# Six weight blocks of the closing MLP prepared at the hand-over instead of during the attention's second half

## The chip, the cores and the metric

The kernel runs on one core of one Trainium2 chip. The metric is the device time of one execution in microseconds (us). A core has TensorE for matmuls (PE in the profile, its weight loads PEld), VectorE (DVE), ScalarE (ACT), GpSimd (POOL) and SyncE (SP), which here only issues DMAs. Each engine works through its own instructions in the order in which they were written, and waits at an instruction until what it needs is there.

## The reference

Attention that keeps the 32 largest scores of each row, then a mixture of experts with one expert for each token, then an MLP with three weight matrices of which the largest product counts:

```
scores = scale * q @ k.T                        # 4 batches, 8 heads, 576 x 576, head size 64
kth    = 32nd largest of each row
attn   = softmax(where(scores >= kth, scores, -1e9)) @ v
x      = attn as [2304, 512]
out    = x;  for tokens with x @ w_skip > 0:  e = argmax(x @ w_gate)
         out += gate * (relu(x @ w1[e]) @ w2[e])            # 8 experts, 512 -> 1024 -> 512
h      = max(out @ m1, out @ m2, out @ m3)                  # 512 -> 768, given as 64-bit floats
y      = h @ m_out                                          # 768 -> 512
```

The weights m1, m2, m3 and m_out reach the chip as 64-bit floats.

## The kernel before

**Stages.** The tokens are worked in two parts of two batches. Attention is a run of 16 jobs (a batch and a pair of heads); each job is five units, a tail unit T of 64 rows for both heads and units 0 to 3 of 128 rows, and takes nine slots. Jobs 0 to 7 are part 0 (slots 0 to 71, `PART1` is 72), jobs 8 to 15 part 1 (slots 72 to 143, `NI` is 144). For each unit PE makes the scores (`scores2`), ACT copies half of them (`copy2`), DVE finds the 32nd largest (`search`, with `folds` and `finds`), ACT and POOL mask and take the exponential (`below`, `mask`, `expo`), PE transposes (`turn`) and multiplies with v (`av`). In part 0 the scores are one product and `scores2` puts two idle matmuls ahead of them (`warm`); in part 1 they are three products of split operands.

**What sets the order.** There is no scheduler. `at(i, o, fn)` puts a step into slot i at place o (0 to 99) and the steps are written out in that order. The table `WHEN`, one for each part, holds for each kind of step its distance in slots from its unit. `search` stands at place 40 of its slots, so the slots go by at the pace of DVE, or of what DVE waits for.

**Fillers.** From slot `b0` on, the expert products of part 0 are dealt out between the attention's steps (`experts`, `filler`): the first step of that list that PE does is `u_x`, which transposes the rows `xg` of the first expert. These rows are gathered by token: `route(0)` finds where each token goes, POOL scatters the rows to `xs` in DRAM (`scatter`), SP reads `xg` back. `BD` sets how many slots lie between the scatters and `b0`; `FLO` is the place in a slot at which the copies that the fillers have left over are made (`flush`).

**Preparation of weights.** The MLP's weights are 24 blocks of 128 x 512 values of 64 bits. `prep_load` brings one in; `prep` turns it into two fp32r tiles, a high and a low half: a square on ACT, four operations on DVE that build a 32-bit float out of the two words, and `split`, which rounds (on ACT) and subtracts (on POOL). `PREP0` and `PREPD` set at which slot the first block is prepared and how many slots lie between two. Blocks 0 to 11 are prepared in the attention's second half, 12 to 23 later.

**The hand-over.** When the attention ends, the first three token tiles of part 0 (`g00`) go on to the MLP: `g_load` gathers the experts' outputs (`yg<-ys`, a DMA that POOL issues once the last expert's output is in DRAM), `g_add` adds them on DVE (`x<-yg,gwc,x`), `g_in` transposes on PE and splits on ACT and DVE (x1h, x1l), and `g_l1` multiplies, with blocks 0 to 5 for its first two columns of blocks and 6 to 11 for the third. Then part 1 is routed, its experts run, and the MLP for the rest.

Of the kernel before, what the change touches and what calls it, by code (L numbers as in the profile page):

```python
# [31 lines left out]
PARTS_ENG = lambda nc: (nc.vector,) * 4  # L32
PARTS_AT = (1, 4, 6)
PARTS_LAST = (1, 0)
FLO = 25
FLE = 25
SPLIT = (1,)
NXR = 1
NLO = 2
SCT = 0.72  # L40
BD = 2
FO = [(50, 1), (90, 99)]
SOON = 0
SC0 = 4
# [2 lines left out]
NM0 = 12  # L47


WHEN = [  # L50
    {"trk": -7.7, "outk": -6.84, "trq": -5.82, "outq": -5.5, "below0": 1.19, "below1": 1.25, "mask0": 1.23,
     "mask1": 1.33, "exp0": 2.36, "exp1": 3.11, "norm": 2.64, "turnT": 3.52, "avT": 4.43, "outT": 5.49,
# [3 lines left out]
    {"trk": -6.4, "outk": -6.07, "trq": -5.4, "outq": -4.92, "below0": 1.15, "below1": 1.25, "mask0": 1.31,  # L56
     "mask1": 1.33, "exp0": 2.15, "exp1": 2.74, "norm": 2.65, "turnT": 3.51, "avT": 4.65, "outT": 5.0,
# [3 lines left out]
]  # L61
BF16 = mybir.dt.bfloat16
PREP0, PREPD, PREP_O = 18, 4, 42
DR_LD = (0, 32)
DR_ADD = (3, 42)
DR_IN = (4, 52)
DR_F = (0, 1, 2)
DR_FS = [(5, 58, 1), (6, 45, 2)]
C2 = (1.125 * 2.0 ** -15) ** 2
# [28 lines left out]
def body(ctx, tc, q, k, v, w_skip, w_gate, w1, w2, m1, m2, m3, m_out, out):  # L98
# [734 lines left out]
    def split(dsth, dstl, src, eng, rnd=None):  # L833
        if rnd:
            rnd.tensor_copy(dsth, src)
        else:
            A.copy(dsth, src)  # L837
        eng.tensor_tensor(dstl, src, dsth, op=ALU.subtract)
# [8 lines left out]
    def place(i, dt=F32):  # L847

        pool = env["M0" if i < NM0 else "M1"]
        Ms[i] = pool.tile([P, 2, 512], dt, name=f"M{i}", bufs=1)  # L850
        return Ms[i]

    def M(x, i):

        return Ms[i][:, x]
# [5 lines left out]
    def prep(i, alone=False):  # L861

        raw = Ms[i].rearrange("p x n -> p (x n)")
        words = raw.bitcast(I32).rearrange("p (n t) -> p n t", t=2)
        w = un.tile([P, 512], F32, name="pw", bufs=3)
        sq = un.tile([P, 512], BF16, name="psq", bufs=3)
        wi = w.bitcast(I32)


        return [  # L870
            lambda: A.activation(sq, raw.rearrange("p (n t) -> p n t", t=2)[:, :, 1], AF.Square),
            lambda: V.tensor_scalar(wi, words[:, :, 1], 5, 2, op0=ALU.logical_shift_left, op1=ALU.logical_shift_right),
            lambda: V.scalar_tensor_tensor(wi, words[:, :, 1], -1073741824, wi, op0=ALU.bitwise_and, op1=ALU.bitwise_or),
            lambda: V.scalar_tensor_tensor(wi, words[:, :, 0], 29, wi, op0=ALU.logical_shift_right, op1=ALU.bitwise_or),
            lambda: V.scalar_tensor_tensor(w, sq, C2, w, op0=ALU.is_ge, op1=ALU.mult),
            lambda: place(i, F32R),
            lambda: split(M(0, i), M(1, i), w, *((V, V) if alone else (G,)))]
# [34 lines left out]
    def g_l1(g, f, M):  # L912

        n = g.n
        pw = []

        def prod(i):
            if i == 0:
                pw.extend(mm3([n * P]))
            ps = pw[i]  # L920
            for c in range(4):
                j = (f // 2) * 6 + i * 2 + c // 2
                o = (c % 2) * 256 + (f % 2) * P
                gh = g.xh[:, c].rearrange("p a b -> p (a b)")[:, 0:n * P]
                gl = g.xl[:, c].rearrange("p a b -> p (a b)")[:, 0:n * P]
                T.matmul(ps, M(0, j)[:, o:o + P], gh, start=(c == 0), stop=False)  # L926
                T.matmul(ps, M(0, j)[:, o:o + P], gl, start=False, stop=False)  # L927
                T.matmul(ps, M(1, j)[:, o:o + P], gh, start=False, stop=(c == 3))  # L928

        def put():  # L930
            mv = env["m2a"].tile([P, GMAX * P], F32, name="mv", bufs=1)[:, 0:n * P]
            A.copy(mv, pw[0])
            V.tensor_max(mv, mv, pw[1])  # L933
            V.tensor_max(mv, mv, pw[2])  # L934
            pool = env["m2a" if f < 3 else "m2"]
            hh = pool.tile([P, GMAX * P], F32R, name=f"h2h{f}", bufs=1)
            hl = pool.tile([P, GMAX * P], F32R, name=f"h2l{f}", bufs=1)
            split(hh[:, 0:n * P], hl[:, 0:n * P], mv, V)
            g.h.append((hh, hl))
        return [lambda: prod(0), lambda: prod(1), lambda: prod(2), put]  # L940
# [29 lines left out]
    NI = i0  # L970
    PART1 = sum(J.n for J in jobs if J.part == 0)

    with tc.manual_schedule():
# [16 lines left out]
        def at(i, o, fn, *a):  # L990
            todo.setdefault(i, []).append((o, len(todo.get(i, [])), fn, a))

        ends = [jobs[-1], [J for J in jobs if J.part == 0][-1]]
        for J in jobs:
# [15 lines left out]
            for u in J.units:  # L1010
                i = z + J.tiles.index((u, 0))
# [45 lines left out]
        fill = experts([0, 1])  # L1057
        b0, b1 = r0 + SC0 + 1 + BD, NI + BX

# [25 lines left out]
        for i in range(b0, b1):  # L1085
            at(i, FLO if i < NI - 3 else FLE, flush)
            for fo, j in FO:
                at(i, fo, filler, i, j, fo == FO[0][0])
        at(2, 39, load_gate)
        def prep_at(i, z):  # L1090
            ops = []
            at(z, PREP_O - 1, lambda: ops.extend(prep(i)))
            for j in range(7):
                at(z + j // 2, PREP_O + j % 2, lambda j=j: ops[j]())

        for i in range(NM0):
            at(PART1 + PREP0 - 6 + PREPD * i, 5, prep_load, i)
            prep_at(i, PART1 + PREP0 + PREPD * i)
        m2a = []

        def turnover():
# [9 lines left out]
                    fsq.pop(0)()  # L1111

        at(NI, 50, turnover)
        at(NI + DR_ADD[0], DR_ADD[1], g_add, g00)
        at(NI + DR_IN[0], DR_IN[1], g_in, g00)
        at(NI + DR_IN[0], DR_IN[1] + 1, lambda: fsq.extend(x for f in DR_F for x in g_l1(g00, f, M)))
        for i, o, n in DR_FS:
# [216 lines left out]
```

## Time and profile before

| | |
|---|---|
| device time, median of 3 runs | 1092.09 us (1091.97 to 1093.41) |
| the profiled execution | 1092.1 us, span 1090.2 us |
| busy: PE, DVE, ACT, POOL | 980.3, 744.0, 592.0, 366.9 us |
| one job in part 0 (148.2 to 182.4 us) | 34.2 us, DVE busy 33.65 |
| attention's second half from the first expert's transposes to PE's last matmul | 361.6 to 639.1 us |
| hand-over, PE idle | 639.1 to 645.1 us |

A busy time is the sum of an engine's instructions as the profiler saw them, overlaps counted once. The granted clock is TensorE's: 1.00 stands for 2.4 GHz and 0.50 for 1.2 GHz, and a mean between them says that the stretch had both. "Idle before" an instruction is the time its engine stood still ahead of it, with the instruction or DMA whose end released it.

### The profile page before, as it was taken

To read this page: it belongs to the slowest core of one execution; us is meant where nothing else is said; L and a number is where in the kernel's file an instruction comes from. 1 tells how busy PE (TensorE), PEld (TensorE's weight loads), DVE (VectorE), ACT (ScalarE), POOL (GpSimd) and SP (SyncE) were. 2 spreads that over 40 slices of the span, in tenths; PEclk is the share of its full clock that TensorE was granted. 3 is DMA by queue.
4 is the path that set the end of the run, shared out by engine and by line. 5 is a ranking of instruction groups with operands and counts; after the bars stand their busy time and mean duration, and the time that the engine had idled before them with its cause. 6 is when DMAs were issued, how large, how long until landed. Compare 5 with 4: busy or idle time off the path is not lost. (4 is left out here: it accounts for less than half of the span.)

```text
span 1090.2 us, 19236 instructions
## 1 busy us (share of the span) xinstructions
PE 980.3 (90%) x6747; PEld 765.5 (70%) x6747; DVE 744.0 (68%) x2482; ACT 592.0 (54%) x1295; POOL 366.9 (34%) x484
## 2 busy tenths in 40 slices
PE   5987788888887889999999978889999999999996
PEld 2554455454554767767677758879889999999995
DVE  5999999999889789999999922774441313222221
ACT  3787878877875777977886831355321211121111
POOL 1444444544455654755654524020030101010000
PEclk8899999989877899999999979899999999999998
DMA  4110111101427566575574556899931111111001
GB/s 115 60 45 16 30 44 45 44 12 34 135 68 227 172 207 198 159 235 178 160 214 148 163 160 213 292 370 370 377 133 58 39 50 49 39 51 36 29 2 32
DMA packets 146154, 136.64 MB, mean 125 GB/s; under 512 B 64384, under 2 KB 110976, under 8 KB 146048
## 3 DMA queue, kind: packets, MB, share of 16 engines
q1 hardware_dynamic: 143168, 125.88, 36.7%
q0 software_dynamic: 2880, 9.44, 2.6%
q8 instruction: 55, 0.90, 0.3%
q14 instruction: 51, 0.42, 0.1%
HBM read 112.22 MB, written 23.07 MB: 124 GB/s over the span
## 5 line engine op out<-in xcount | busy, mean ns | idle before, releaser
L442 POOL TENSOR_TENSOR e<-sc,e 128x576 f32<-128x576 f32 x144 | 201.6, 1416 | 93.0 <-ACT e L437 91.5
L926 PE MATMUL pe<-x1h,M 128*128 128x384 f32 x432 | 145.8, 338 | 0.0
L928 PE MATMUL pe<-x1h,M 128*128 128x384 f32 x432 | 145.2, 336 | 0.0
L927 PE MATMUL pe<-x1l,M 128*128 128x384 f32 x432 | 145.2, 336 | 0.0
L475 PE MATMUL pe<-ident,e 128*128 128x128 f32 x624 | 106.4, 291 | 35.9 <-POOL e L460 16.1
L730 PE MATMUL pe<-xT,raw 128*128 128x128 f32 x1024 | 127.6, 280 | 1.7 <-ACT xT L719 1.1
L730 PEld LDWEIGHTS pe<-xT,raw 128*128 128x128 f32 x1024 | 121.4, 195 | 6.0 <-issue 2.8
L933 DVE TENSOR_TENSOR mv<-mv,pe 128x384 f32<-128x384 f32 x36 | 19.9, 554 | 151.9 <-PE pe L928 143.8
L475 PEld LDWEIGHTS pe<-ident,e 128*128 128x128 f32 x624 | 70.6, 145 | 74.9 <-ACT e L451 22.1
L437 ACT ACTIVATE e<-sc,sts 128x576 f32<-128x576 f32 x144 | 111.4, 779 | 16.1 <-POOL sts L418 15.9
L476 ACT COPY et<-pe 128x384 f32<-128x384 f32 x208 | 97.9, 480 | 39.2 <-PE pe L475 38.4
L451 ACT ACTIVATE e<-e,sts 128x576 f32<-128x576 f32 x144 | 113.6, 789 | 4.1 <-POOL e L442 4.0
L837 ACT CAST h2h<-mv 128x384 fp32r<-128x384 f32 x36 | 18.5, 514 | 147.8 <-DVE mv L934 141.9
L494 PE MATMUL pe<-et,ldv 128*64 128x128 f32 x1024 | 84.4, 294 | 7.0 <-ACT et L476 7.0
L418 POOL TENSOR_TENSOR sts<-g,stc 128x4 f32<-128x4 f32 (+1 forms) x80 | 20.2, 253 | 191.6 <-DVE g L395 170.1
L494 PEld LDWEIGHTS pe<-et,ldv 128*64 128x64 f32 x1024 | 64.5, 145 | 28.3 <-ACT et L476 19.5
L384 DVE MATCH_REPLACE8 g<-g 128x144 f32<-128x144 f32 x288 | 82.6, 293 | 0.0
L926 PEld LDWEIGHTS pe<-x1h,M 128*128 128x128 f32 x432 | 81.7, 189 | 0.5 <-issue 0.2
L927 PEld LDWEIGHTS pe<-x1l,M 128*128 128x128 f32 x432 | 81.6, 189 | 0.4 <-issue 0.2
L928 PEld LDWEIGHTS pe<-x1h,M 128*128 128x128 f32 x432 | 81.6, 189 | 0.0
L746 PE MATMUL pe<-raw,hT 128*128 128x512 f32 x160 | 78.5, 605 | 1.5 <-ACT et L476 1.0
L383 DVE MAX8 g<-g 128x8 f32<-128x144 f32 x288 | 74.9, 297 | 0.0
(223 smaller groups left out, 2044.6 us busy)
## 6 DMA issues: line engine op xcount, KB each, us to landing
raw<-in_moe_w_dram SPq DMA_DIRECT2D x128, 512.0 KB, 5.4
M<-in_moe_w_dram SPq DMA_DIRECT2D x18, 512.0 KB, 5.2
M<-xd SPq DMA_DIRECT2D x18, 256.0 KB, 5.4
x<-xd SPq DMA_DIRECT2D x18, 256.0 KB, 3.6
ldq<-in_q_dram SPq DMA_DIRECT2D x32, 128.0 KB, 3.3
ldk<-in_k_dram SPq DMA_DIRECT2D x32, 128.0 KB, 2.8
ldv<-in_v_dram SPq DMA_DIRECT2D x32, 128.0 KB, 2.6
xs<-zerob SPq DMA_DIRECT2D x16, 256.0 KB, 2.8
```

Of the source, the lines that this page charges most:

```text
L384: ops += [lambda h=h, o=o: V.match_replace(g[:, h, 0:QS], g[:, h, o:o + 8], g[:, h, 0:QS], NEG) for h in range(nh)]
L437: A.activation(J.w[i], J.sc[i], AF.Relu, bias=J.st[i][0], scale=-BIG)
L442: G.tensor_tensor(w, J.sc[i], w, op=ALU.subtract)
L451: A.activation(J.w[i], J.w[i], AF.Exp, bias=J.st[i][1], scale=0.125, accum_out=J.ss[:, j:j + 1])
L475: T.transpose(pe[:, i], e[:, 3 * g + i], ident)
L476: A.copy(et[:, 3 * g:3 * g + 3], pe[:, 0:3])
L494: T.matmul(xo[h * 64:(h + 1) * 64], vt[:, i, h, :], et[:, 5 * h + i], start=(i == 0), stop=False)
L730: T.matmul(u.ph[:, f], u.c1[2 * n + f // 2][:, c, (f % 2) * P:(f % 2 + 1) * P], u.xT[:, c], start=(c == 0), stop=(c == 3))
L746: T.matmul(u.py, x, w[:, ws], start=(c + a + j == 0), stop=(c + a == 4 and j == len(prods) - 1))
L926: T.matmul(ps, M(0, j)[:, o:o + P], gh, start=(c == 0), stop=False)
L927: T.matmul(ps, M(0, j)[:, o:o + P], gl, start=False, stop=False)
L928: T.matmul(ps, M(1, j)[:, o:o + P], gh, start=False, stop=(c == 3))
```

## The change

Blocks 0 to 5 stay in the attention's second half, every eighth slot instead of every fourth. Blocks 6 to 11 are loaded in slots 130 to 135 and prepared at the hand-over in two groups of three (`DR_PREP`, `pre`): the squares, then the four DVE operations, then place and split, with rounding and subtraction both on DVE (`prep(i, True)`). `g_in` comes one slot earlier (`DR_IN`), the fillers begin one slot earlier (`BD`), `flush` stands at place 15 instead of 25, and 30 numbers of `WHEN` move, among them in part 0 the third transposition of a unit (turn2), the tail's scores (s0T) and products (avT).

```
-FLO = 25
+FLO = 15
-BD = 2
+BD = 1
...
-     "turn0": 3.21, "turn1": 3.361, "turn2": 4.37, "av": 4.95, "rows1": 3.43, "rows2": 5.51, "rows3": 6.05,
+     "turn0": 3.21, "turn1": 3.361, "turn2": 3.52, "av": 4.95, "rows1": 3.93, "rows2": 5.51, "rows3": 5.97,
...
-PREP0, PREPD, PREP_O = 18, 4, 42
+PREP0, PREPD, PREP_O = 20, 8, 42
+DR_PREP = [[(-1, 12), (0, 42), (0, 43), 6, 9], [(2, 21), (2, 44), (3, 43), 9, 12]]
-DR_IN = (4, 52)
+DR_IN = (3, 52)
...
-        for i in range(NM0):
+        for i in range(6):
             at(PART1 + PREP0 - 6 + PREPD * i, 5, prep_load, i)
             prep_at(i, PART1 + PREP0 + PREPD * i)
+        for i in range(6, NM0):
+            at(NI - 20 + i, 5, prep_load, i)
+
+        def pre(a, b):
+
+            ops = []
+
+            def first():
+                ops.extend([prep(i, True) for i in range(a, b)])
+                for o in ops:
+                    o[0]()
+
+            def rest(rs):
+                for r in rs:
+                    for o in ops:
+                        o[r]()
+            return first, lambda: rest(range(1, 5)), lambda: rest((-2, -1))
+
...
+        for *places, a, b in DR_PREP:
+            for (i, o), fn in zip(places, pre(a, b)):
+                at(NI + i, o, fn)
```

**DVE at the hand-over.** Before, the last search (MAX) is followed at once by the three additions of `g_add`; rs and lt belong to the last job, x1l to `g_in`.

```order
L395 MAX g<-g 128x8 x2
L899 SCALAR_TENSOR_TENSOR x_8019<-yg,gwc_100,x_8019 128x512
L899 SCALAR_TENSOR_TENSOR x_8023<-yg,gwc_100,x_8023 128x512
L899 SCALAR_TENSOR_TENSOR x_8027<-yg,gwc_100,x_8027 128x512
L454 TENSOR_SCALAR rs<-ss 128x8
L455 RECIPROCAL rs<-rs 128x8
L838 TENSOR_TENSOR x1l<-pe,x1h 128x4x128 x3
```

In the changed program the whole of blocks 6 to 8 and the four operations of blocks 9 to 11 stand between the last search and the additions; here are the rows from the last of those operations on.

```order
L876 SCALAR_TENSOR_TENSOR pw<-psq,pw 128x512 x3
L900 SCALAR_TENSOR_TENSOR x_7987<-yg,gwc_100,x_7987 128x512
L900 SCALAR_TENSOR_TENSOR x_7991<-yg,gwc_100,x_7991 128x512
L900 SCALAR_TENSOR_TENSOR x_7995<-yg,gwc_100,x_7995 128x512
L836 CAST M_8052<-pw 128x512
L839 TENSOR_TENSOR M_8052<-pw,M_8052 128x512
L836 CAST M_8053<-pw 128x512
L839 TENSOR_TENSOR M_8053<-pw,M_8053 128x512
L836 CAST M_8054<-pw 128x512
L839 TENSOR_TENSOR M_8054<-pw,M_8054 128x512
L839 TENSOR_TENSOR x1l<-pe,x1h 128x4x128 x3
```

Thirty DVE operations moved ahead of the additions (three times four and three times two for blocks 6 to 8, three times four for 9 to 11), and six stand between the additions and x1l.

**PE at the first expert's transposes.** xg are the rows that SP reads back after the scatters; s and sa are score tiles. Before, two sets of scores, each behind its two idle matmuls on zerob, stand ahead of them, with the transposes of q (ldq) between the two sets; the second set and what follows are:

```order
L316 LDWEIGHTS zerob
L316 MATMUL sa<-zerob 128x512
L316 LDWEIGHTS zerob
L316 MATMUL sa<-zerob 128x512
L291 MATMUL sa<-kt,qt 128x288
L291 MATMUL sa<-kt,ql 128x288
L291 MATMUL sa<-kl,qt 128x288
L291 MATMUL sa<-kt,qt 128x288
L291 MATMUL sa<-kt,ql 128x288
L291 MATMUL sa<-kl,qt 128x288
L475 MATMUL pe<-ident,e 128x128 x3
L717 MATMUL pe<-ident,xg 128x128 x4
```

In the changed program the same place reads:

```order
L243 MATMUL pe<-ident,ldk 128x128 x4
L245 MATMUL pe<-ident,ldk 128x64
L476 MATMUL pe<-ident,e 128x128 x6
L718 MATMUL pe<-ident,xg 128x128 x4
L292 MATMUL s<-kt,qt 128x288
L292 MATMUL s<-kt,ql 128x288
L292 MATMUL s<-kl,qt 128x288
L292 MATMUL s<-kt,qt 128x288
L292 MATMUL s<-kt,ql 128x288
L292 MATMUL s<-kl,qt 128x288
L243 MATMUL pe<-ident,ldq 128x128 x4
L245 MATMUL pe<-ident,ldq 128x128
```

The transposes of xg moved ahead of both sets of scores and of the transposes of q; the idle matmuls on zerob are gone there.

**PE at the hand-over.** The rows on e, et and ldv are the last units' `turn` and `av`, those on x are `g_in`. Before:

```order
L475 MATMUL pe<-ident,e 128x128 x9
L494 MATMUL pe<-et,ldv 64x128 x8
L497 MATMUL pe<-et,ldv 64x128 x2
L909 MATMUL pe<-ident,x_8019 128x128 x4
L909 MATMUL pe<-ident,x_8023 128x128 x4
L909 MATMUL pe<-ident,x_8027 128x128 x4
L519 MATMUL pe<-ident,xt 128x128
```

In the changed program:

```order
L476 MATMUL pe<-ident,e 128x128 x9
L910 MATMUL pe<-ident,x_7987 128x128 x4
L910 MATMUL pe<-ident,x_7991 128x128 x4
L910 MATMUL pe<-ident,x_7995 128x128 x4
L495 MATMUL pe<-et,ldv 64x128 x8
L498 MATMUL pe<-et,ldv 64x128 x2
L520 MATMUL pe<-ident,xt 128x128
```

The last `av` of the attention moved from ahead of `g_in` to behind it.

## Rows read from the trace of the kernel before

**Rows 1.** The page, busy time of each engine over the span.

```profile
PE 980.3 (90%) x6747; PEld 765.5 (70%) x6747; DVE 744.0 (68%) x2482; ACT 592.0 (54%) x1295; POOL 366.9 (34%) x484
```

**Rows 2.** Stretches: from:to, length, busy time of each engine, PEclk, DMA share, GB/s.

```profile
148.20:182.40 34.20, 28.34 (x228) 17.04 (x226) 33.65 (x131) 27.44 (x64) 16.45 (x24) 1.00 0.15 35
217.00:253.60 36.60, 30.99 (x230) 18.66 (x226) 34.05 (x131) 27.80 (x64) 16.54 (x24) 0.91 0.14 34
253.60:292.00 38.40, 32.50 (x233) 19.99 (x229) 35.15 (x131) 28.95 (x69) 20.17 (x28) 0.87 0.13 31
331.50:379.75 48.25, 37.71 (x273) 26.15 (x270) 39.60 (x174) 29.62 (x71) 28.87 (x45) 0.75 0.58 188
361.60:639.10 277.50, 263.19 (x2189) 195.53 (x2188) 252.22 (x887) 218.43 (x504) 151.10 (x187) 0.99 0.60 185
587.30:639.10 51.80, 51.73 (x426) 38.06 (x425) 38.86 (x144) 36.34 (x81) 21.32 (x28) 1.00 0.60 185
...
645.10:720.00 74.90, 65.37 (x378) 60.35 (x379) 43.45 (x106) 22.93 (x38) 19.27 (x27) 0.87 0.70 243
```

**Rows 3.** Groups of DVE, 380 to 626.6 us: busy us, mean ns | idle before.

```profile
L873 DVE SCALAR_TENSOR_TENSOR pw<-M,pw 128x512 int32<-128x512 int32 x12 | 11.3, 943 | 0.0
...
L874 DVE SCALAR_TENSOR_TENSOR pw<-M,pw 128x512 int32<-128x512 int32 x12 | 8.4, 703 | 0.4
L875 DVE SCALAR_TENSOR_TENSOR pw<-psq,pw 128x512 f32<-128x512 bf16 x12 | 8.3, 691 | 0.1
...
L872 DVE TENSOR_SCALAR pw<-M 128x512 int32<-128x512 int32 x12 | 7.2, 602 | 0.0
```

**Rows 4.** Waits of PE, 361.6 to 640 us: total us, times, longest.

```profile
PE pe L475 <- POOL e L460: 4.8, 5, 1.5
PE s L291 <- DVE g L381: 4.4, 8, 1.2
```

**Rows 5.** Timeline of PE, 350 to 362 us: start, us, instruction, count.

```profile
353.81 1.03 PE L316 MATMUL s<-zerob 128*128 128x512 bf16 x2
354.78 0.61 PE L291 MATMUL s<-kt,qt 64*128 64x288 f32 x2
...
356.92 0.89 PE L316 MATMUL sa<-zerob 128*128 128x512 bf16 x2
357.74 0.41 PE L291 MATMUL sa<-kt,qt 64*128 64x288 f32 x2
...
358.11 0.31 PE L291 MATMUL sa<-kl,qt 64*128 64x288 f32 x2
...
360.74 0.93 PE L717 MATMUL pe<-ident,xg 128*128 128x128 f32 x4 [0.58 <-DMA xg<-xs]
```

**Rows 6.** Timeline of DVE at the hand-over, and three blocks prepared later.

```profile
625.82 0.82 DVE L395 MAX8 g<-g 128x8 f32<-128x296 f32 x2
644.19 0.75 DVE L899 SCALAR_TENSOR_TENSOR x<-yg,gwc,x 128x512 f32<-128x512 f32 x1 [17.56 <-DMA yg<-ys,srcm]
...
649.32 0.69 DVE L838 TENSOR_TENSOR x1l<-pe,x1h 128x512 fp32r<-128x512 f32 x1 [0.21 <-ACT x1h L837]
...
702.12 1.09 DVE L872 TENSOR_SCALAR pw<-M 128x512 int32<-128x512 int32 x3
...
706.74 1.89 DVE L875 SCALAR_TENSOR_TENSOR pw<-psq,pw 128x512 f32<-128x512 bf16 x3
```

**Rows 7.** Timeline of PE at the hand-over.

```profile
626.43 1.09 PE L494 MATMUL pe<-et,ldv 128*64 128x128 f32 x16
...
637.12 1.64 PE L494 MATMUL pe<-et,ldv 128*64 128x128 f32 x16
638.69 0.44 PE L497 MATMUL pe<-et,ldv 64*64 64x128 f32 x4
645.09 2.22 PE L909 MATMUL pe<-ident,x 128*128 128x128 f32 x8 [5.96 <-DVE x L899]
```

**Rows 8.** Timeline of POOL at the hand-over: the first gather.

```profile
640.20 1.05 POOL L891 DMA_INDIRECT yg<-ys,srcm  x1 [7.35 <-DMA ys<-yo]
```

More of the change, by code (lines that the diff above doesn't have):

```diff
@@ L50 @@
 WHEN = [
-    {"trk": -7.7, "outk": -6.84, "trq": -5.82, "outq": -5.5, "below0": 1.19, "below1": 1.25, "mask0": 1.23,
-     "mask1": 1.33, "exp0": 2.36, "exp1": 3.11, "norm": 2.64, "turnT": 3.52, "avT": 4.43, "outT": 5.49,
[3 rows of a table removed]
-    {"trk": -6.4, "outk": -6.07, "trq": -5.4, "outq": -4.92, "below0": 1.15, "below1": 1.25, "mask0": 1.31,
-     "mask1": 1.33, "exp0": 2.15, "exp1": 2.74, "norm": 2.65, "turnT": 3.51, "avT": 4.65, "outT": 5.0,
[3 rows of a table removed]
+    {"trk": -7.77, "outk": -6.88, "trq": -5.82, "outq": -5.2, "below0": 1.19, "below1": 1.25, "mask0": 1.23,
+     "mask1": 1.29, "exp0": 2.36, "exp1": 3.11, "norm": 2.94, "turnT": 3.52, "avT": 5.39, "outT": 5.45,
[3 rows of a table added]
+    {"trk": -6.32, "outk": -5.92, "trq": -5.44, "outq": -5.0, "below0": 1.15, "below1": 1.29, "mask0": 1.31,
+     "mask1": 1.33, "exp0": 2.15, "exp1": 2.74, "norm": 2.65, "turnT": 3.51, "avT": 4.8, "outT": 5.0,
[3 rows of a table added]
 ]
 BF16 = mybir.dt.bfloat16
-PREP0, PREPD, PREP_O = 18, 4, 42
+PREP0, PREPD, PREP_O = 20, 8, 42
+DR_PREP = [[(-1, 12), (0, 42), (0, 43), 6, 9], [(2, 21), (2, 44), (3, 43), 9, 12]]
 DR_LD = (0, 32)
 DR_ADD = (3, 42)
-DR_IN = (4, 52)
+DR_IN = (3, 52)
 DR_F = (0, 1, 2)
```

10 rows, old and new, of the table WHEN are left out of this document.

## The prediction

> **What bounds the kernel now.** I read the stretches first, engine by engine, since the share of busy time over the whole span hides stages with different limits: PE is busy for 90% of it and DVE for 68% [rows 1], but not together. A job in the middle of part 0 takes 34.20 us and DVE is busy for 33.65 of them, at a granted clock of 1.00 [rows 2]: there DVE sets the pace and PE (28.34) has room. Two later jobs of part 0 take 36.60 and 38.40 us; the clock was 0.91 and 0.87, and DVE, with about the same work (34.05 and 35.15), waits 2.6 and 3.3 us [rows 2]. The job from 331.5 to 379.75 us, in which part 0 is routed and scattered, has a clock of 0.75, and DVE stands still for 8.65 us of it [rows 2].
>
> From the first expert's transposes to PE's last attention matmul (361.6 to 639.1 us, 277.5 us) two engines are nearly full: DVE 252.2 us, all of it before 626.6, and PE 263.2 us [rows 2]. PE's idle time is therefore 277.5 - 263.2 = 14.3 us. The waits name what ends it: POOL's normalised tail (4.8 us) and DVE's release of the score tile (4.4 us) come first [rows 4]. In the last 51.8 us of it PE has no idle time worth the name (51.73 busy) [rows 2]: it is behind all the others there. ACT (218) and POOL (151) bound nothing.
>
> At the hand-over DVE ends its last search at 625.82 + 0.82 = 626.6 us and then stands still until 644.19, 17.6 us, for the gathered expert outputs [rows 6]. Their gather could be issued only at 640.20, when the last expert's output was in DRAM [rows 8]; that output is PE's work, so PE's end of the fillers, not DVE's of the searches, starts this chain. PE itself is done at 639.1 and idle until 645.09 [rows 7]. In the 74.9 us that follow PE is busy for 65.4 [rows 2]; then it is the bound to the end. So a microsecond that PE gains before 720 us is one that the kernel gains.
>
> **Taken out of the second half.** Twelve blocks cost DVE 11.3 + 8.4 + 8.3 + 7.2 = 35.2 us between 380 and 626.6 us, 2.93 each [rows 3]; three blocks at a quieter place take 702.12 to 708.63, 2.17 each [rows 6]. Six blocks fewer are thus worth 13.0 to 17.6 us of DVE. I take 16, near the upper end, because its rows are those of this very stretch, less some overlap between neighbours. The squares and roundings that leave ACT, and the subtractions that leave POOL, are worth nothing: both have over 50 us of room [rows 2].
>
> What DVE gives, PE must be able to take. PE's work doesn't shrink, so the stretch can't lose more than PE's idle 14.3 us, and 16 is more than that: PE becomes the bound of the second half. What stays of the idle time has two ends: 0.4 us, if all of the stretch were like its last fifth (0.07 in 51.8), and 4.8 us, if the waits for the normalised tail stay. I take 1.5, nearer the first, because an engine that is behind finds its operands ready. Gain: 14.3 - 1.5 = 12.8 us.
>
> **Fillers one slot earlier.** The first filler step on PE, the transposes of xg, now stands ahead of two sets of scores and the transposes of q. Before, xg let PE go on at 360.74 [rows 5]. The scatters behind it are POOL's and keep their slots, so I take this time as it is. PE then reaches the transposes where its idle matmuls began, at 353.8 us, and stands for 6.9 us. What it did meanwhile comes after: 354.78 to 356.92 and 357.74 to 358.42, together 2.8 us [rows 5] (the idle matmuls are dropped). At the full clock it would be some 2.1 us (the same product took 0.61 us first and 0.41 later in these rows). If the pause keeps the clock at half for ten more microseconds, that ratio of 1.5 adds 3.3 us: 6.1. I take 2.8. The scores come some 7 us later to DVE, which is idle for 8.65 us in this job already; what it waits more there is the same loss, not a second one.
>
> **The other moved steps.** In part 1 they move by less than half a slot, apart from one of ACT's copies (c0T), a slot later. They and the earlier flush are covered by PE being behind: 0; without that cover they cost what such waits cost before, at most 1.5 us a time [rows 4]. In part 0 the pace is DVE's and its work is the same: 0 at a full clock. The clock there is a rival, below.
>
> **Added at the hand-over.** On DVE each block costs 2.17 us for the four operations [rows 6]. The rounding has no row on DVE; between the integer operation, 0.36 us (1.09 for three), and the subtraction x1l, 0.69 [rows 6], I take 0.5. The subtraction from two tiles lies between 0.63 (1.89 for three) and 0.69: 0.65 [rows 6]. Six blocks: 6 x 3.3 = 20 us. Thirty operations, 13.0 + 3 x 1.15 = 16.5 us, stand ahead of the additions. The wait of 17.6 us hides them, with 1.1 us to spare if DVE keeps its distance to the gather; DVE, no longer the bound, can only be further ahead. Cost 0; without the cover each microsecond of delay is one of the additions, of x1h and x1l and of the MLP's first products. The blocks themselves are needed only by the third column, after two that use blocks 0 to 5.
>
> The other 3.5 us stand between additions and x1l. Over the same time PE has something new: the attention's last `av`, which was done at 637.12 to 639.13, just ahead of the pause [rows 7], and now stands behind `g_in`'s transposes, ahead of the last job's. Nothing hides it there: 2.0 us, by the row itself; 1.4 if it runs as at 626.43 (1.09 us and its short rest) [rows 7]; 3.5 if x1l is what PE waits for. I take 2.0.
>
> **Sum.** -12.8 + 2.8 + 2.0 = -8.0 us. The profiled execution took 1092.1 us, 1.9 more than its span, and is the median of the runs (1092.09). 1092.1 - 8.0 = **1084.1 us**. With the ends of the terms, 1081.7 (0.4, 2.1, 1.4) to 1092.2 (4.8, 6.1, 3.5); nearly all of its chance lies below 1089.
>
> **Rivals.**
>
> *DVE's time comes through whole.* If PE's busy time holds slack that a faster DVE uncovers, the stretch loses all 16 us and the pause for xg is swallowed: 1092.1 - 16 + 2.0 = 1078.1. For it: weight loads were busy for only 195.5 of the 277.5 us [rows 2]. Against it: PE's rows stand end to end in the last 51.8 us, and DVE's end there didn't help it. The Trainium skill, "Trainium Kernel Development and Optimization", section Performance Expectations, says that matmul busy time is a bad measure of how close one is to the limit and weight loads a good one; by that rule this rival would be the forecast. The trace agrees with it only so far: weight loads leave room, but the rows of PE's last stretch leave no gap.
>
> *Part 0 keeps its clock.* In part 0 the third transposition comes earlier and the tail's scores fill the slot that it leaves. If PE's work is thereby more even, the two jobs at 0.91 and 0.87 could run like the one at 1.00: 36.6 + 38.4 - 2 x 34.2 = 6.6 us less [rows 2], 1077.5. For it: the loss is there only with the lower clock. Against it: the jobs before had the same steps and kept 1.00, so evenness alone isn't it.
>
> *The second half's gain is eaten at the hand-over.* If DVE leaves the searches late, since it now waits for PE's scores, the block of 16.5 us reaches past the gather: with 4 us of delay, and x1l 1.5 later than PE, 1084.1 + 5.5 = 1089.6; between 1087 and 1093 with less or more. Three gathers of about 1 us would then be issued beside it; beside POOL's work one of these operations took 943 ns on average, against 630 at the quiet place [rows 3, 6], so these two do hold each other up. The Trainium skill, "SBUF — State Buffer", section SBUF: two separate sides, warns of just this: a DMA issued by GpSimd waits for its descriptors while DVE copies fp32 between SBUF tiles, 3100 ns where 620 would do. By it the three gathers would come some 7.5 us later, an estimate from that page; no run here shows a gather beside such a copy.
>
> *Slower: part 0 loses its clock.* The re-placed steps may thin out a stretch of PE's work that was just enough. Jobs 1 to 5 ran at about 34.2 us; if each goes like the two at 0.91 and 0.87 (37.5 on average), that is 5 x 3.3 = 16.5 us: 1084.1 + 16.5 = 1100.6. It decides from the third such job on (8.0 + 2.2 us). For it: the drop does happen in this part with hardly any change in PE's work (28.3 against 31.0 busy). Against it: the tail's scores move into PE's emptier slots.
>
> *The change does not shorten the second half.* If PE's gaps only move (another engine ends them), the pause and the `av` remain: 1092.1 + 2.8 + 2.0 = 1096.9. Against it: the two largest waits are DVE's, directly or through the tail's norm.
>
> **How the numbers follow.** The forecast 0.40, DVE's time whole 0.15, part 0 with a full clock 0.13, eaten at the hand-over 0.12, part 0 slower 0.14 (a fifth of it mild, within the bound), no shorter second half 0.06. A change of 0.2% (2.2 us) is about what a measurement of this kernel can tell. Faster: 0.40 + 0.15 + 0.13 + half of 0.12 = 0.74; the same: the other half and the mild part, 0.09; slower: 0.11 + 0.06 = 0.17. The range from 1075 to 1094 leaves out the slower cases above (0.15) and a little below.
>
> **What the profile would show.** Right: from PE's first transposes of xg to its last `av` some 10 us less, PE idle there under 3 us and DVE with waits of over 10 us for scores or their copies; PE waiting some 7 us at the first transposes of xg; DVE's preparation done before the first addition, which still waits for the gather; `av` after `g_in`. Wrong: additions that start straight after a preparation; job lengths in part 0 other than 34.2 us up to 217 us, with a clock below 1.00; or a stretch that shrinks by more than PE's idle time.

## The result and the profile after

The changed kernel takes 1086.12 us (median of 6 runs, 1083.16 to 1090.29), the kernel before 1093.43 beside it (6 runs, 1091.97 to 1098.16). The ratio of the two is 0.991, with a 95% interval from 0.989 to 0.993 (the medians alone give 0.993). The changed kernel is faster, by 7.3 us in the medians; 8.0 less was forecast, 1084.1 us. The sum came out; most of its terms did not, as the traces and the experiments show. The profiled execution is the longest of the six (1090.29 us, span 1088.5), so it shows losses larger than the median has. Lines from 64 on stand one lower than before (L718 was L717).

Busy times over the span, as in [rows 1]:

```profile
PE 960.5 (88%) x6708; PEld 763.4 (70%) x6745; DVE 751.6 (69%) x2494; ACT 587.7 (54%) x1289; POOL 368.4 (34%) x478
```

Stretches of the changed kernel, with the columns of [rows 2]: four jobs of part 0, the job with the routing, from the first xg transposes to PE's last turn, and the hand-over in two pieces, up to the first addition and from there to the first xg of part 1.

```profile
147.06:181.03 33.97, 26.38 (x226) 16.81 (x226) 33.59 (x131) 27.19 (x64) 16.47 (x23) 1.00 0.15 36
215.42:249.80 34.38, 26.40 (x226) 16.81 (x226) 33.90 (x132) 27.30 (x64) 16.47 (x23) 1.00 0.15 36
249.80:284.94 35.14, 27.40 (x231) 18.19 (x232) 34.66 (x131) 28.92 (x69) 19.86 (x27) 0.95 0.14 33
284.94:323.46 38.52, 29.20 (x255) 20.21 (x255) 35.48 (x140) 28.46 (x69) 19.88 (x27) 0.87 0.47 150
323.46:374.67 51.21, 35.62 (x280) 27.14 (x282) 39.71 (x175) 29.96 (x71) 29.21 (x44) 0.77 0.55 181
...
352.55:628.22 275.67, 265.66 (x2192) 198.51 (x2192) 253.83 (x887) 214.61 (x495) 149.44 (x182) 0.98 0.62 187
628.22:637.53 9.31, 0.00 (x0) 0.00 (x0) 5.71 (x10) 2.17 (x5) 7.26 (x3) 0.71 0.39 118
...
637.53:680.23 42.70, 36.66 (x203) 34.22 (x204) 19.32 (x60) 6.86 (x14) 14.22 (x24) 0.82 0.45 157
```

The reader is to see three things. First, the two jobs of 36.60 and 38.40 us in [rows 2] take 34.38 and 35.14, and the routing starts at 323.46 instead of 331.5: 8 us are won before any weight block is prepared. The job with the routing takes 51.21 instead of 48.25 us, 3.0 more. And the second half has become shorter by little: from the first xg transposes to the last turn 275.67 us (before, by [rows 5, 7], from 360.74 to 637.12, where the av that moved begins: 276.4), with 10.0 us of PE idle in it where 1.5 were forecast. Part of that is the pause: the scores that were pushed behind it now lie in this window. From the end of the job with the routing to the last turn, without them, it is 253.55 us (374.67 to 628.22) against 257.37 before (379.75 to 637.12), 3.8 less.

What PE waits for from 340 to 640 us, answering to [rows 4], and what DVE waits for from 353 to 616 us:

```profile
PE pe L910 <- DVE x L900: 10.7, 2, 10.2
PE pe L718 <- ACT et L477: 7.1, 1, 7.1
PE pe L476 <- POOL e L461: 4.2, 3, 2.1
...
PE s L292 <- DVE g L382: 2.0, 2, 1.1
```

```profile
DVE qa L378 <- ACT sc L333: 13.6, 10, 2.5
```

The pause at the first xg transposes is there (7.1 us; 6.9 forecast), and DVE waits for scores as forecast. (The row names ACT's copy of et as what ended the pause; it ended at 352.53, and about then, some 2.9 us after their read was issued at 349.72, the rows xg landed.) But the wait for POOL's normalised tail, of which little was to be left, is still 4.2 us.

The hand-over on POOL and on DVE, answering to [rows 8] and [rows 6]:

```profile
615.66 6.72 POOL L419 TENSOR_TENSOR sts<-g,stc 128x4 f32<-128x4 f32 x1 [1.76 <-PE pe L747]
...
629.49 5.36 POOL L892 DMA_INDIRECT yg<-ys,srcm  x1 [3.00 <-issue]
635.16 0.95 POOL L892 DMA_INDIRECT yg<-ys,srcm  x1 [0.30 <-issue]
```

```profile
627.42 1.09 DVE L873 TENSOR_SCALAR pw<-M 128x512 int32<-128x512 int32 x3
628.43 1.89 DVE L874 SCALAR_TENSOR_TENSOR pw<-M,pw 128x512 int32<-128x512 int32 x3
630.24 1.89 DVE L875 SCALAR_TENSOR_TENSOR pw<-M,pw 128x512 int32<-128x512 int32 x3
632.04 1.89 DVE L876 SCALAR_TENSOR_TENSOR pw<-psq,pw 128x512 f32<-128x512 bf16 x3
637.53 0.75 DVE L900 SCALAR_TENSOR_TENSOR x<-yg,gwc,x 128x512 f32<-128x512 f32 x1 [3.60 <-DMA yg<-ys,srcm]
```

The preparation does end before the first addition, and the addition still waits for its gather, as forecast. But the gather's issue took 5.36 us where it took 1.05 [rows 8]: it lies beside DVE's nine operations with two tiles and ends 0.9 us after the last of them, about the time that it takes by itself. The same happened at 615.66 to a small operation of POOL (`stats`, sts: the largest and the 32nd largest score of each row of the last unit, times constants; 128 x 4 values, called row sums in the expectations below). It took 0.20 us for the unit before.

### The profile page after: what moved, and what is told of

Its sections match the earlier page's. It is cut to its first block, busy times and chain, and to the rows that moved or that the text cites. A ratio compares the mean times of both kernels' runs of the same rounds, so it can differ in the third digit from the quotient of the medians.

```text
span 1088.5 us, 19221 instructions
## 1 busy us (share of the span) xinstructions
PE 960.5 (88%) x6708; PEld 763.4 (70%) x6745; DVE 751.6 (69%) x2494; ACT 587.7 (54%) x1289; POOL 368.4 (34%) x478
## 5 line engine op out<-in xcount | busy, mean ns | idle before, releaser
L476 PE MATMUL pe<-ident,e 128*128 128x128 f32 x624 | 100.6, 287 | 26.6 <-ACT e L452 18.2
L419 POOL TENSOR_TENSOR sts<-g,stc 128x4 f32<-128x4 f32 (+1 forms) x80 | 24.8, 310 | 186.4 <-DVE g L396 156.8
L495 PE MATMUL pe<-et,ldv 128*64 128x128 f32 x1024 | 74.9, 287 | 4.0 <-ACT et L477 4.0
L892 POOL DMA_INDIRECT yg<-ys,srcm x18 | 22.5, 1247 | 153.9 <-DVE x L900 146.9
```

What stands on the lines that cost most here:

```text
L476: T.transpose(pe[:, i], e[:, 3 * g + i], ident)
```

## Two theories

**Theory 1**, the prediction's: the gain is DVE's relief in the second half. **Theory 2**: it comes from the re-placed steps of part 0, and what the move of the six blocks wins in the second half is given back at the hand-over, where DVE's preparation holds POOL. Ratios are to the kernel before, on the same chip; its median there was 1096.12 us for the first four kernels, 1095.74 for the next four and 1094.13 for the last four.

## First experiments: the move and the steps apart

**The move alone.**

```diff
(the changed kernel, with all of WHEN as before, and)
-FLO = 15
+FLO = 25
-BD = 1
+BD = 2
```

> The change without its re-placed steps: blocks 6 to 11 at the hand-over and g_in a slot earlier, but WHEN, FLO and BD as before. Theory 1 (the prediction's: the gain is DVE's relief in the second half): the terms -12.8 and +2.0 stand alone, without the 2.8 of the earlier fillers, so -10.8 us, a ratio of 0.990, and PE's idle time from the first xg transposes to its last turn falls from 14.3 to under 3 us. Theory 2 (the gain is the re-placed steps', above all those of part 0, and DVE's preparation at the hand-over holds up POOL there): the second half gains 1 to 4 us and the hand-over loses 5 to 7, so +1 to +6 us, 1.001 to 1.006, with a first gather (POOL) of about 5 us and the last unit's row sums (POOL, 128x4) of several us.

**The steps alone.** The kernel before with the change's WHEN, FLO = 15 and BD = 1.

> The kernel before with the re-placed steps alone (WHEN, FLO 15, BD 1); all twelve blocks prepared in the second half as before. Theory 1: the pause at the first xg transposes costs 2.8 us and nothing else changes: +2.8 us, a ratio of 1.003. Theory 2: part 0 gains about 8 us, the pause takes 3 back, the second half is as before: -5 to -8 us, 0.993 to 0.995, with the hand-over's first gather at about 1 us.

**Part 0's steps alone.** The kernel before with the change's first row of WHEN, and nothing else.

> The kernel before with the new row of WHEN for part 0 alone; FLO, BD, the row for part 1 and the preparation as before. Theory 1: DVE sets the pace of part 0 and its work is the same, so no change, 0.999 to 1.001. Theory 2: the scores and transpositions of part 0 fill PE more evenly, the clock is at half for less of part 0's last jobs, and the searches of part 1 begin about 8 us earlier: -6 to -9 us, 0.992 to 0.995, and the second half keeps its 277.5 us.

**The changed kernel again.**

> The changed kernel once more, for a second profile beside the first, which was its slowest run. Theory 1: the second half is shorter by more than in the first profile (by 5 us or more against 277.5), and that makes the difference between 1090 and the median of 1086. Theory 2: the second half is again within 2 us of before, the hand-over again has a first gather of about 5 us, and what differs between the profiles is how much of part 0 runs at the lower clock.

Measured:

| kernel | median us | ratio | 95% |
|---|---|---|---|
| move alone | 1096.18 | 0.9998 | 0.998 to 1.002 |
| steps alone | 1090.07 | 0.9949 | 0.993 to 0.997 |
| part 0's steps alone | 1086.06 | 0.9909 | 0.988 to 0.994 |
| the changed kernel | 1087.01 | 0.9923 | 0.990 to 0.995 |

Theory 1 falls: the move alone is worth nothing, and part 0's row alone is worth all of the change. Where the move's gain goes is read from its stretches: up to the last search, up to the last turn, then the hand-over in its two pieces.

```profile
361.46:620.77 259.31, 250.16 (x2104) 189.64 (x2104) 237.70 (x867) 206.84 (x476) 139.18 (x178) 0.98 0.62 188
...
361.46:633.56 272.10, 261.31 (x2172) 196.25 (x2172) 250.39 (x887) 214.81 (x495) 149.28 (x182) 0.98 0.62 189
633.56:642.68 9.12, 0.00 (x1) 0.00 (x0) 5.57 (x11) 2.34 (x5) 6.21 (x3) 0.75 0.45 144
642.68:685.86 43.18, 37.01 (x203) 34.57 (x204) 17.39 (x52) 6.32 (x13) 14.22 (x24) 0.82 0.46 156
```

Up to the last search DVE is busy for 237.70 us instead of 253.1 (from 360.74 on, of which [rows 2] have 252.22): 15.4 less, as forecast. But the searches end only 6.6 us sooner (259.31 against 626.64 - 360.74 = 265.9) and the last turn 4.3 us sooner (272.10 against 276.4), and PE keeps 272.10 - 261.31 = 10.8 us of idle time. The hand-over then takes 9.12 + 43.18 = 52.3 us, before 45.4 (from 637.12 to 644.19 [rows 6, 7] and from there to the first xg of part 1 at 682.55): 6.9 us more, 2.1 of them ahead of the first addition and 4.8 behind it, where the clock was 0.82 and before 0.86. -4.3 + 6.9 is a small loss in this execution and nothing in the median. What DVE gained, it waited away:

```profile
DVE qa L378 <- ACT sc L333: 14.9, 10, 2.9
```

Before, the wait for these copies was 5.9 us over the same stretch. PE waits there for POOL's tail (3.2 us), for DVE's release of the score tile (2.9) and in five shorter waits: no one engine is behind the others throughout; they wait for each other in turn.

The same stretches for part 0's steps alone, whose second half and hand-over are those of before:

```profile
353.28:628.14 274.86, 261.82 (x2173) 194.57 (x2173) 251.98 (x886) 217.38 (x501) 150.84 (x187) 0.99 0.62 185
628.14:635.27 7.13, 1.97 (x20) 1.17 (x20) 0.00 (x0) 0.94 (x3) 2.93 (x3) 0.95 0.69 234
635.27:674.98 39.71, 34.10 (x183) 32.77 (x184) 13.99 (x46) 6.06 (x12) 14.24 (x25) 0.84 0.50 169
```

The steps alone lose 4 us against part 0's steps alone: the job with the routing takes 51.20 instead of 47.90 us (the pause), and from its end to the last turn there are 260.96 us (376.01 to 636.97) instead of 257.44 (370.70 to 628.14). So without the relief on DVE, what else the steps change (part 1's new places, the earlier flush and what the earlier fillers do later, which no run takes apart) costs some 3.5 us there.

The second profile of the changed kernel (1085.4 us) has 273.44 us from xg to the last turn, a first gather of 5.73 us and `stats` of 6.73, as the first has. Neither theory named what differs: the stretch from the first addition to part 1's first xg took 38.75 us at a clock of 0.90, in the first profile 42.70 at 0.82. That is 4.0 of the 4.9 us between them, and PE's busy time in it, 33.27 against 36.66 us, is most of the difference.

## What in part 0 gains: three numbers

**The tail's numbers**, eleven of the sixteen that move in part 0's row, the six larger ones of them here:

```diff
-"norm": 2.64, "avT": 4.43, "rows1": 3.43, "s0T": -3.57, "c0T": -3.4, "rows2e": 5.26
+"norm": 2.94, "avT": 5.39, "rows1": 3.93, "s0T": -4.57, "c0T": -3.9, "rows2e": 5.41
```

> The kernel before with those numbers of part 0's row of WHEN that concern the tail unit and the rows (avT, s0T, c0T, norm, rows1, rows2e and five small ones); turn2, s0, c0, mask1 and c1 stay. Theory A: part 0's gain of about 10 us comes from DVE no longer waiting for PE's router products (2.1 and 2.5 us in the two jobs before the routing), because the tail's products no longer stand ahead of rows2: then this kernel shows most of it, 0.993 or less, and no wait of lt for PE in these jobs. Theory B: it comes from the earlier third transposition and the later scores, which spread PE's work and keep its clock: then this kernel is within 0.998 to 1.001, and lt still waits for 2 us or more a job.

Measured: 1086.06 us, 0.9918 (0.989 to 0.994). Theory A. The number of the tail's steps that it takes was then cut to three:

```diff
-"avT": 4.43, "s0T": -3.57, "c0T": -3.4
+"avT": 5.39, "s0T": -4.57, "c0T": -3.9
```

> The kernel before with three numbers changed: avT 5.39, s0T -4.57 and c0T -3.9 of part 0's row, so that in every job the tail's products and its scores no longer stand between the transpositions and rows2 on PE. Theory A in its narrow form (these two, at 1 us each at the lower clock, are what lt waited for): lt waits for under 1 us in the two jobs before the routing, part 0 gains about as much as with the whole row, 0.991 to 0.993. If the other steps of the tail (norm, rows1) are needed as well: 0.995 to 0.998.

Measured: 1086.09 us, 0.9922 (0.990 to 0.995): with three numbers the whole effect. The place is the same in every job. PE in the kernel with the move alone, whose part 0 is that of before:

```profile
239.54 1.92 PE L495 MATMUL pe<-et,ldv 128*64 128x128 f32 x16
...
242.01 0.95 PE L476 MATMUL pe<-ident,e 128*128 128x128 f32 x6
242.89 0.69 PE L486 MATMUL pe<-et,ldv 128*64 128x64 f32 x16
243.51 0.33 PE L489 MATMUL pe<-et,ldv 64*64 64x64 f32 x4
243.77 0.60 PE L317 MATMUL sa<-zerob 128*128 128x512 bf16 x2
244.21 0.65 PE L292 MATMUL sa<-kt,qd 128*128 128x288 f32 x2
244.70 0.27 PE L520 MATMUL pe<-ident,xt 128*128 128x128 f32 x1
```

And with the three numbers:

```profile
237.18 0.88 PE L475 MATMUL pe<-ident,e 128*128 128x128 f32 x6
237.89 0.27 PE L519 MATMUL pe<-ident,xt 128*128 128x128 f32 x1
```

Between the transpositions of e and those of xt (`rows2`) stood the tail's products (L486, L489) and its scores with their idle matmuls (sa): 244.70 - 242.89 = 1.8 us. `rows2` makes the router's products, which DVE scales (lt), and DVE, which sets the pace, waits for them. DVE's waits in the two jobs from 217 to 292 us (36.60 and 38.40 us in [rows 2]) in the kernel before, the same in the kernel with the move alone, then those of the kernel with the three numbers over these two jobs and the next:

```profile
DVE lt L539 <- PE pe L526: 4.6, 2, 2.5
```

```profile
DVE lt L540 <- PE pe L527: 4.5, 2, 2.5
```

```profile
DVE lt L539 <- PE pe L526: 1.6, 2, 0.9
```

From the first search to the routing the time falls from 319.4 to 310.0 us, 9.4, and DVE's idle time in it from 13.8 to 6.4; its waits for lt there fall from 6.9 to 1.6 (the other 2.0 us are busy time of DVE). A better clock is not what does it in the first of the two jobs: that job takes 34.40 us at 0.95 here and took 34.38 at 1.00 in the changed kernel. The next section's kernel has the new order too, and its earlier jobs ran at 0.90:

```profile
112.84:147.13 34.29, 29.64 (x230) 18.36 (x226) 33.91 (x132) 27.00 (x64) 16.40 (x24) 0.90 0.18 42
```

At such a clock the order before was late by 2 us (36.60 us at 0.91 [rows 2]); the new one has that to spare. In the second of the two jobs the clock still counts: 35.14 us at 0.95 and 36.90 at 0.91 in the changed kernel's two profiles.

## The pause at the first expert

```diff
-BD = 1
+BD = 2
```

> The changed kernel with BD back at 2, so that the fillers begin a slot later; FLO, both rows of WHEN and the preparation at the hand-over as in the change. The prediction's step: the pause at the first xg transposes and the 2.8 us of scores pushed behind it go away, -2 to -3 us against the changed kernel, a ratio to before of about 0.989 to 0.990, and PE waits there for under 2 us instead of 7. Rival: the list of fillers then has one slot less, PE is the bound afterwards, and the time is the same as the changed kernel's, 0.991 to 0.993.

Measured: 1086.19 us, 0.9918 (0.989 to 0.994), as the changed kernel. The job with the routing takes 48.70 us (51.21 and 49.70 in the changed kernel's two profiles) and PE waits 2.0 us at xg. Its `stats` took 6.74 us as before, but its first gather only 1.17, though it too was issued beside the nine operations; the additions then began 18.3 us after the last search instead of 22.0, as soon as DVE was through with the preparation. So the pause costs 1 to 3 us where it stands, but undoing it does not show in the total; the interval of some 3 us to either side doesn't settle whether the later fillers take it back.

## What holds POOL at the hand-over

The same work, written block by block in `pre`:

```diff
                 def rest(rs):
-                for r in rs:
-                    for o in ops:
+                for o in ops:
+                    for r in rs:
                         o[r]()
```

> The changed kernel with DVE's work at the hand-over written block by block instead of operation by operation: of each block one operation with a single tile as source, then three with two, in place of three, then nine in a row. The work is the same. If POOL is held for as long as operations with two tiles stand back to back on DVE: POOL's row sums of the last unit take at most 2.2 us instead of 6.7, the first gather at most 3 us instead of 5.4 to 5.7, the first addition comes 3 to 4 us sooner after the last search, and the time falls by 2 to 4 us against the changed kernel. If POOL is held by all of DVE's work, or by something else: the 6.7 and 5.7 us stay, and so does the time.

> The move of the six blocks alone (all re-placed steps as before), with DVE's work at the hand-over written block by block. The move alone had 0.9998. If its gain in the second half (4 to 6 us) was eaten by POOL's being held behind DVE's long stretches of operations with two tiles: 3 to 5 us come back, 0.995 to 0.997, and the first gather takes 1.1 us instead of 4.3. If the hold cost nothing in the end: 1.000. Theory 1's 10.8 us would be 0.990.

> A candidate: part 0's row of WHEN from the change, part 1's row, FLO and BD from before, and the six blocks at the hand-over written block by block. Theory 2 with POOL held for less: part 0 gives 10 us, the move 2 to 4 us more since the hand-over loses 3 to 4 us less than in the move alone, so 0.987 to 0.989. If the hold isn't shortened: as with part 0's row alone, 0.990 to 0.992. Theory 1 (the move is worth 10.8 us by itself): 0.981.

Measured: the change with this order 1084.46 us, 0.9901 (0.987 to 0.993); the move alone with it 1095.04 us, 1.0004 (0.999 to 1.002); part 0's steps and the move with it 1082.35 us, 0.9897 (0.987 to 0.993). None of the three shows the gain that was expected clear of its interval. POOL in the second of these:

```profile
621.25 0.30 POOL L419 TENSOR_TENSOR sts<-g,stc 128x4 f32<-128x4 f32 x1 [2.35 <-PE pe L747]
...
636.70 1.05 POOL L892 DMA_INDIRECT yg<-ys,srcm  x1 [7.72 <-issue]
638.05 1.39 POOL L892 DMA_INDIRECT yg<-ys,srcm  x1 [0.30 <-DVE pw L874]
```

For `stats` it is shown that the order of DVE's work holds POOL: 6.72 us became 0.30, with the same work in another order. What in the order does it is not. In the old order (the changed kernel) `stats`, begun at 615.66, was through at 622.38; in the new one, begun at 621.25, at 621.55. DVE beside the one and beside the other:

```profile
615.49 1.08 DVE L873 TENSOR_SCALAR pw<-M 128x512 int32<-128x512 int32 x3
...
621.90 0.43 DVE L836 CAST M<-pw 128x512 fp32r<-128x512 f32 x1
```

```profile
621.09 0.40 DVE L873 TENSOR_SCALAR pw<-M 128x512 int32<-128x512 int32 x1
621.53 0.72 DVE L874 SCALAR_TENSOR_TENSOR pw<-M,pw 128x512 int32<-128x512 int32 x1
```

In the old order three operations with one source, back to back, stand at the head of the run, and they did not let `stats` through either. In the new order each operation of a block waits for the one before it, and a gap of 0.04 us stands between the first and the second. So it can be the two tiles or the missing gaps; no run takes these apart. The first gather's 4.31 us became 1.05; that fits, but with BD at 2 it was short in the old order too. The price was mis-stated, though: the time of the move alone did not fall. DVE now is what the additions wait for:

```profile
641.31 0.69 DVE L876 SCALAR_TENSOR_TENSOR pw<-psq,pw 128x512 f32<-128x512 bf16 x1
641.92 2.28 DVE L900 SCALAR_TENSOR_TENSOR x<-yg,gwc,x 128x512 f32<-128x512 f32 x3
```

They follow the last preparation without a gap, 20.7 us after the last search (621.2); with the gather held they came 21.9 us after it, before 17.6. (In the change itself it is 20.9 against 22.0 us; 3 to 4 us sooner were expected.) The prediction's block of 16.5 us is 18.4 in the old order (620.8 to 639.1 in the move alone) and 20.8 in this one, both longer than their cover of 17.6. About 2 us of either lie beside POOL's masks, where some of DVE's operations of 0.69 us took 1.71 and more. The new order adds the rest: a block's four operations take 2.59 us when each waits for the one before it (634.16 to 636.75 here), and 2.14 when three blocks take turns (615.49 to 621.90 for three in the changed kernel). So what POOL gains by this order, DVE loses: the gather is 3.3 us shorter and the block 2.4 us longer.

Stretches of the third kernel: to the last turn, to the first addition, to part 1's first xg.

```profile
351.87:621.49 269.62, 259.68 (x2172) 194.79 (x2172) 249.20 (x880) 213.93 (x493) 142.01 (x181) 0.99 0.63 189
621.49:630.24 8.75, 0.01 (x1) 0.00 (x0) 8.20 (x15) 2.34 (x5) 3.16 (x3) 0.61 0.66 217
630.24:671.43 41.19, 36.01 (x203) 34.17 (x204) 19.25 (x61) 6.83 (x14) 14.22 (x24) 0.83 0.45 158
```

Against part 0's steps alone: 5.2 us less in the second half, 1.6 + 1.5 more at the hand-over. The 2 us that are left don't show: 0.9897 lies just above the 0.987 to 0.989 expected, and its interval holds the 0.9909 of part 0's steps alone.

## Two attempts on what is left

On top of that third kernel, first the av back ahead of `g_in`, then also blocks 9 to 11 wholly behind `g_in`:

```diff
-DR_IN = (3, 52)
+DR_IN = (4, 52)
```

> The candidate of the last run with g_in a slot later (DR_IN (4, 52)), so that the attention's last av stands ahead of g_in's transposes again, in PE's wait. The prediction's term of 2.0 us for this av: the first MLP product follows the first addition after 7.5 to 8 us instead of 9.6, and the time falls by 2 us against the candidate, a ratio to before of 0.986 to 0.988. Rival: the six roundings and subtractions and x1l, which stay behind the additions on DVE, take the place of the av as what PE waits for, and the time stays at 0.989 to 0.990.

```diff
-... [(2, 21), (2, 44), (3, 43), 9, 12]]
+... [(2, 21), (4, 54), (4, 55), 9, 12]]
```

> The last one, and blocks 9 to 11 wholly behind g_in on DVE, so that the additions wait for their gather alone. If DVE's second group holds up the additions (they started 0.0 us after it in the candidate, and 3.5 us after the gather's usual landing in the kernel with the block order alone): the first addition comes 1 to 2 us earlier after the first gather and the time falls by as much, 0.985 to 0.987. Rival: the 11 us of preparation then stand ahead of the routing's small operations and PE waits for these after the first MLP column, and the time is the same or up to 3 us longer than without it.

Measured: 1083.25 us, 0.9890 (0.987 to 0.991), and 1083.65 us, 0.9894 (0.987 to 0.992): no gain from either, and both rivals came true. With the av ahead, the first MLP product follows the first addition after 9.29 us (9.56 without), since PE waits for x1l behind the six roundings and subtractions; with the group behind, after 7.69, but then PE waits for the routing's operations on DVE, which stand behind that group (L597 is the routing's first product). PE's waits of the one and of the other:

```profile
PE pe L521 <- DVE x1l L839: 2.5, 1, 2.5
```

```profile
PE pe L597 <- DVE mv L935: 5.5, 1, 5.5
```

The three kernels with part 0's steps and the block order lie at 1082.4 to 1083.7 us, 0.989 to 0.990: below both kernels of this study by their medians, but their intervals overlap the changed kernel's (0.989 to 0.993), so that they beat it isn't settled.

## Why the prediction was right, and where only its sum was

Set against the forecast, the terms are these, in us, by the two profiles of the changed kernel (1090.29 and 1085.38 us) and the one of before (1092.1):

| | forecast | first | second |
|---|---|---|---|
| part 0, to the start of the routing | 0 | -8.0 | -6.7 |
| job with the routing: the pause | +2.8 | +3.0 | +1.5 |
| from there to the last turn | -12.8 | -3.8 | -4.6 |
| from there to part 1's first xg | +2.0 | +6.6 | +2.8 |
| sum | -8.0 | -2.2 | -7.0 |
| the execution's time | | -1.8 | -6.7 |

**"In part 0 the pace is DVE's and its work is the same: 0 at a full clock"** is the step that failed. Part 0's steps are worth 8 to 10 us. The pace was DVE's, but DVE had 13.8 us of idle time between its first search and the routing, and half of it was a wait for PE's lt that three of the moved numbers end. The prediction saw the idle 2.6 and 3.3 us of the two jobs in [rows 2] and put them down to the clock, without reading what DVE waited for there. That wait stood in the trace of before.

**Second half, -12.8 us.** DVE's share was right (15.4 us against 16, within 13.0 to 17.6). "PE becomes the bound" was not: PE kept 10.8 us of idle time, far beyond the upper bound of 4.8. Measured from the first xg to the last turn: -4.3 (the move alone), -5.1 (with the block order), -5.2 (with part 0's steps). The sentence that fails is that an engine that is behind finds its operands ready: DVE and PE wait for each other in turn through the score tiles and the tail's norm, and of the 15.4 us taken from DVE, 9 came back as its own waits for scores (5.9 before, 14.9 then).

**Pause at xg, +2.8 us.** Right where it stands: 7.1 us of pause, 3.0 and 1.5 us in that job (3.3 between the two kernels without the move). In the total it could not be resolved.

**The other moved steps, 0.** In part 1 not contradicted under its condition, that PE is behind. Without the relief on DVE, the stretch behind the job with the routing took 3.5 us more.

**Hand-over, +2.0 us.** It cost 6.9 us in the move alone, 4.6 with the block order (8.72 + 41.28 us against 45.4). "The wait of 17.6 us hides them, with 1.1 us to spare" fails on its own size first: the block took 18.4 us, since DVE's operations were slowed beside POOL's masks, and 20.8 in the block order. On top of that the gather was held in three profiles. Both are what the rival "eaten at the hand-over" expected of DVE and POOL side by side; its first link, that DVE leaves the searches late, was wrong: DVE left them sooner. What the later additions cost in the end isn't settled. Behind the first addition the stretch to part 1's first xg goes with the clock more than with any order: 42.70 and 38.75 us in the two executions of the changed kernel at 0.82 and 0.90, 38.36 before at 0.86, 37.42 at 0.94 in the change with the block order. The 2.0 for the av came to 1.8 (9.56 us from addition to MLP product, against 7.72 with part 0's steps alone), but it isn't recovered by moving the av back, and in the changed kernel's two profiles this distance was 10.60 and 8.95, so its size is open.

The Trainium skill, "SBUF — State Buffer", section SBUF: two separate sides, says that DVE and GpSimd share a port pair that whoever starts first holds alone for the whole instruction; a DVE operation with two inputs in SBUF is among them, against a GpSimd operation that reads SBUF. For `stats` the traces agree that the other blocks, but it took 6.72 to 6.74 us in all four profiles with the old order, so that it got through not after one instruction but after the whole run. For a DMA that GpSimd issues, the same section infers that a tensor_tensor, with both of its inputs in SBUF, does not hold it up. Here the operations are of the kind scalar_tensor_tensor, with two tiles: three of the four gathers were held (4.31, 5.36 and 5.73 us), the fourth (1.17 us) was not.

**The rivals.** DVE's time whole: excluded, the second half gave a third of it. Part 0 keeps its clock: right in place and nearly in size (6.6 us), but the lever was the order on PE, which no longer needs the better clock in the first of the two jobs. Part 0 slower: didn't occur (its bound of 10.2 us needs four jobs at 3.3 us, not three). No shorter second half: it became shorter by 3.8 to 4.6 us behind the job with the routing.

So the sum was right by errors that cancelled: 7 to 10 us in part 0 that were not in it, against 8 to 9 us too many in the second half and 1 to 5 too few at the hand-over. With the move alone, the same working would have given 1081.3 us for a kernel that measured no change.

## What to carry to other kernels

Where an engine sets the pace and still idles for 2 us in a stretch, read who ends that idle time before calling it the clock; a few numbers that reorder the engine it waits for can be worth more than 15 us of work taken from it. Two engines with 5% of idle time each that feed one another gave back here a third of what one was relieved of, not all of it. And work that is moved into an idle stretch of DVE is not free if POOL has work there: the two slow each other down, and the order that let POOL through made DVE's work longer by nearly as much.

## What the runs showed of the hardware

A run of DVE operations without gaps, three with one source and nine with two tiles, held a POOL operation of 0.20 us for 6.7 us each time. Nine operations with two tiles held a gather's issue of 1.05 us for 4.3 to 5.7 us in three profiles out of four; in the fourth (BD at 2) the gather came through in 1.17 us beside the same nine operations. Why it was let through there is open. Written block by block, with at most three such operations in a row and gaps within a block, the longest hold of a gather was 0.44 us. It goes both ways: beside POOL's mask of 128 x 576, DVE's 0.69 us became 1.71. The clock after PE's pause at the hand-over differed between two executions of the same program, 0.82 and 0.90 up to part 1's first xg, and that stretch took 42.70 and 38.75 us.
